# An attention and feed-forward kernel on one core: first loads in halves, tile 0 in halves, V first, hand-chosen PSUM banks and a new work list

## The chip, the core and the metric

The kernel runs on one core of a Trainium2 chip. The metric is the device time of one execution in microseconds, from the start to the end of the program on the chip; lower is better. A core has a matrix engine (TensorE, PE in the profile; PEld is its weight load), VectorE (DVE), ScalarE (ACT), GpSimd (POOL) and SyncE (SP). Each works through a queue of instructions of its own in order, and waits on semaphores for the others. Sixteen DMA engines move data between the main memory and the on-chip memory SBUF; matrix products land in PSUM.

## What is computed

With x of 2048 rows by 512, everything in bf16 at the inputs:

```python
xn = _layernorm(x, axis=-1)
return x + _A_ref(xn, A_wq, A_wk, A_wv, A_wo, A_beta) + _B_ref(xn, B_w1, B_w2)
```

`_B_ref` is a feed-forward block: `silu(xn @ w1) @ w2`, with 1792 inner columns. `_A_ref` is an attention of 32 heads of width 16 over 4 segments of 512 rows, each with a memory of the segments before:

```python
logits = jnp.einsum('bhqd,bhkd->bhqk', qs, ks) * scale + mask
p = _softmax(logits, axis=-1)
a_dot = jnp.einsum('bhqk,bhkd->bhqd', p, vs)
num = jnp.einsum('bhld,bhde->bhle', pq, M)
den = jnp.einsum('bhld,bhd->bhl', pq, z)[..., None] + 1e-06
o = g * (num / den) + (1.0 - g) * a_dot
M = M + jnp.einsum('bhld,bhle->bhde', pk, vs)
z = z + jnp.einsum('bhld->bhd', pk)
```

`pq` and `pk` are `phi(q)` and `phi(k)`, `phi(t) = t + 1` where t is positive, else `exp(t)`; the outputs of the segments go through `wo`.

## The kernel before, in words

**Tiles.** The 2048 rows are 16 tiles of 128, four to a segment. A row tile is loaded, its mean and variance are taken on VectorE (`ln_sums`, line 286, and `ln_var`, line 289), one over the deviation is a square root on ScalarE (line 303) and a reciprocal on VectorE (line 306) for tiles 0 to 3, a power on GpSimd (lines 297 and 300) for four tiles at once later on. `ln_norm` (line 315) writes the normed tile. It is then transposed into `xnT`: tiles 0 to 3 on TensorE against an identity (`turn_mm`, line 845) with a copy out of PSUM (`turn_copy`, line 851), tiles 4 to 15 by a transposing DMA that SyncE issues (`turn_far`, line 857).

**Products.** k, q and h (the inner feed-forward layer) of a segment are made transposed, 128 of their columns by 512 rows: four passes over the inner dimension of 512. `dense` and `dense_mm` make them in pieces, so that the list can put other work between: for segments 0 and 1 a product has 4 pieces, for 2 and 3 it has 2. In segment 0, `dense` cuts each product into two halves of 256 rows (two pieces each), so that the first half needs only tiles 0 and 1. V is made row tile by row tile (`v_mm`). `product` (lines 336 and 338) issues a pass as one matmul of the whole 128 by 128 array, or as four of 128 rows by 32 columns side by side, when its neighbours are of that tiling.

**Attention.** A "score block" S is 8 to 16 matmuls of 16 or 32 rows (line 724) into four PSUM banks `psS`, and one exponential on ScalarE over 128 by 2048 (line 730), then masks on GpSimd (line 744). There are 72, and one buffer `psS`, so the next block's matmuls wait for the exponential of the one before. E and O (`weigh`, line 791) multiply the weights by V. k needs a copy (line 376) and a split into odd and even heads (`k_split` on GpSimd, or `k_fast`, lines 392 and 393, on VectorE and ScalarE) before the first scores, q a copy (line 399). The other four PSUM banks are a pool with four buffers that take turns (`bank`).

**Output.** `out_mm` adds up 18 passes for an output tile (14 of the feed-forward block, 4 of the attention), in wholes, halves (`oc`), quarters (`od`), and for the last tile in column halves (`oh`); `store` (line 621) and `half_store` (line 668) add x and send the result off.

**Order.** All of this is issued from one list of words, `ORDER`, written out by hand, 1349 words: each word is a function and its arguments (`v0.0.2` is segment 0, tile 0, piece 2 of V; `S0` a score block; `Nv1` the norm of tile 1 on VectorE; `X1.1` its transposes; `Xa1.1` and `Xv2.1` copies on ScalarE and VectorE; `xc`, `xd`, `xq`, `xi` the steps of the statistics; `busy44` 44 fillers, matmuls of zeros that have no use in the result; `tb` a first exponential on one column; `ka`, `kv`, `qa`, `qv`, `va`, `vv` copies on ScalarE or VectorE; `xl` loads of x for the output). The words of one engine run on it in the order of the list. The loads ahead of the list are issued by SyncE and ScalarE in the order of the program: SyncE x tiles 0 and 2, wv in two halves, wk, wq, x tiles 4 to 7, w1 in two halves, x tiles 8 to 11, 12 to 15, beta; ScalarE x tiles 1 and 3.

The tiling of a product's neighbours decides its form, by this table in the last loop:

```python
TILED = {"S": "rows", "E": "cols", "O": "cols", "s": "cols", "m": "cols", "X": "whole", "busy": "whole"}
```

Of the kernel before, what the change touches and what calls it, by code (L numbers as in the profile page):

```python
# [22 lines left out]
S7 xs11 xg8.4 v1.2.0 v1.2.1 v1.2.2 v1.2.3 vv1.2 h0.1.2 h0.1.3 ha0.1 E0  # L23
S5 h0.4.0 h0.4.1 hv0.1 Ev0 h0.4.2 h0.4.3 v1.1.0 v1.1.1 fv0.2 v1.1.2 v1.3.0 fp0.3 ha0.4 v1.1.3 vv1.1
S11 hv0.4 q1.2.0 q1.2.1 q1.2.2 v1.3.1 kind fa0.1 q1.2.3 qv1.2 v1.3.2 v1.3.3 vv1.3 Nv8 XD8 O0 lw0 kp0.3 fv0.0 Ov0
S6 fa0.3 k1.2.0 k1.2.1 k1.2.2 h0.5.0 h0.5.1 h0.5.2 q1.1.0 h0.5.3 ha0.5 k1.2.3 kv1.2 q1.1.1 q1.1.2 hv0.5
S8 h0.7.0 q1.1.3 qv1.1 h0.6.0 h0.6.1 h0.6.2 h0.6.3 ha0.6 fv0.3 E1 Ev1 k1.0.0
S9 hv0.6 h0.7.1 h0.7.2 h0.7.3 Om0 ha0.7 k1.0.1 k1.0.2 kp1.2 q1.0.0 q1.0.1 q1.0.2 fp0.1 Nv9 XD9 xs12 k1.0.3 kv1.0 kp1.0
S10 h0.8.0 hv0.7 h0.8.1 h0.8.2 h0.8.3 ha0.8 h0.9.0 h0.9.1 q1.0.3 t0.3 Nv10 XD10 h0.9.2 h0.9.3 qv1.0
S13 hv0.8 O1 Ov1 xs15 v1.0.0 v1.0.1 v1.0.2 ha0.9 v1.0.3 vv1.0 h0.10.0 h0.10.1 bmask  # L30
S12 k1.1.0 k1.1.1 k1.1.2 t0.2 k1.1.3 kv1.1 h0.10.2 h0.10.3 ha0.10 hv0.9 h1.0.0 Om1 h1.0.1 h1.0.2
# [62 lines left out]
def kernel(  # L94
# [13 lines left out]
    nc = tc.nc  # L108
# [211 lines left out]
    def bank(shape, dtype, name):  # L320
        return pp.tile(shape, dtype, name=name, tag="pb")
# [621 lines left out]
```

## Time and profile before

| what | value |
|---|---|
| time, median of three runs | 220.31 us (220.21 to 221.13) |
| span of the profiled execution, first to last instruction | 218.2 us |
| the profiled execution's own time | not given; the median is 2.1 us above its span |
| TensorE busy | 210.9 us, 97% |
| ScalarE busy | 184.1 us, 84% |
| VectorE busy | 181.3 us, 83% |
| GpSimd busy | 127.4 us, 58% |
| first score block (line 724), start | 11.95 us |
| first exponential of scores (line 730), start | 12.40 us |
| exponentials of scores | 72 of 1.878 us |

A row of the profile's timeline gives the start, the duration, the engine, the line of the kernel, the instruction, what it writes and reads, the shape and how many instructions are merged in it; in brackets stands how long the engine was idle before and what ended that. A row of the stretches gives the window, its length, then for each of TensorE, its weight loads, VectorE, ScalarE and GpSimd the busy time and the number of instructions, then the clock granted to TensorE, the share of the DMA engines and the GB/s moved. The ends of matmuls are modelled and overlap, so a busy TensorE is not one at its peak.

### The profile page before, as it was taken

To read this page: it belongs to the slowest core of one execution; us is meant where nothing else is said; L and a number is where in the kernel's file an instruction comes from. 1 tells how busy PE (TensorE), PEld (TensorE's weight loads), DVE (VectorE), ACT (ScalarE), POOL (GpSimd) and SP (SyncE) were. 2 spreads that over 40 slices of the span, in tenths; PEclk is the share of its full clock that TensorE was granted. 3 is DMA by queue.
4 is the path that set the end of the run, shared out by engine and by line. 5 is a ranking of instruction groups with operands and counts; after the bars stand their busy time and mean duration, and the time that the engine had idled before them with its cause. 6 is when DMAs were issued, how large, how long until landed. Compare 5 with 4: busy or idle time off the path is not lost.

```text
span 218.2 us, 9267 instructions
## 1 busy us (share of the span) xinstructions
PE 210.9 (97%) x3982; PEld 116.1 (53%) x4006; DVE 181.3 (83%) x370; ACT 184.1 (84%) x173; POOL 127.4 (58%) x203
## 2 busy tenths in 40 slices
PE   7899999999999999999999999999999999999994
PEld 7666656655544544455444545445464544465653
DVE  6899999999799899667979886887979897858844
ACT  3799999999999999999999999999989998942000
POOL 6067676789568984697766436962787473410000
PEclk9999999999999999999999999999999999999999
DMA  6996249322200430541125131420042120412223
GB/s 183 344 375 160 51 125 243 74 53 53 51 5 17 157 71 10 117 95 40 49 67 83 54 97 28 74 77 6 0 132 73 52 73 13 131 32 79 84 66 98
DMA packets 33273, 19.60 MB, mean 90 GB/s; under 512 B 14672, under 2 KB 33232, under 8 KB 33232
## 3 DMA queue, kind: packets, MB, share of 16 engines
q1 hardware_dynamic: 30608, 16.39, 28.7%
q10 hardware_dynamic: 2624, 2.62, 3.8%
q8 instruction: 31, 0.51, 1.0%
q14 instruction: 10, 0.08, 0.1%
HBM read 9.96 MB, written 2.10 MB: 55 GB/s over the span
## 4 chain that ended last, share of the span: by engine, by line
PE 92%; DMA 3%; ACT 2%; issue 1%; SPq 1%; DVE 0%
PE ps L336 26%; PE psO L338 17%; PE ps L338 16%; PE psS L724 11%; PE psO L336 9%; PE psV L791 8%; PE psS L338 4%; DMA wk_sb<-in_A_wk_dram 3%; ACT Pb L730 2%; PE psM L452 1%; SPq L169 0%; SPq L158 0%; PE ps L509 0%; ACT th L492 0%; DVE o_half L668 0%
## 5 line engine op out<-in xcount | busy, mean ns | idle before, releaser
L730 ACT ACTIVATE Pb<-psS 128x2048 bf16<-128x2048 f32 x72 | 135.2, 1878 | 4.7 <-PE psS L724 2.4
L744 POOL TENSOR_SCALAR_AFFINE_SELECT Pb<-Pb 128x512 bf16<-128x512 bf16 (+2 forms) x88 | 62.3, 718 | 22.4 <-ACT Pb L730 19.6
L497 DVE SCALAR_TENSOR_TENSOR hT<-th,ps 128x512 bf16<-128x512 bf16 x56 | 38.0, 682 | 10.1 <-ACT th L492 9.4
L744 POOL TENSOR_SCALAR_AFFINE_SELECT lows<-Pb 64x512 bf16<-64x512 bf16 (+1 forms) x40 | 24.3, 607 | 32.0 <-ACT Pb L730 24.9
L338 PE MATMUL psO<-w_sb,hT 128*32 128x512 bf16 (+2 forms) x696 | 41.4, 321 | 0.0
L336 PE MATMUL ps<-xnT,w_sb 128*128 128x512 bf16 (+1 forms) x177 | 35.9, 330 | 0.2 <-issue 0.2
L492 ACT ACTIVATE th<-ps 128x512 bf16<-128x512 f32 x56 | 33.0, 594 | 3.5 <-PE ps L338 3.1
L338 PEld LDWEIGHTS <-hT 128*32 128x32 bf16 x864 | 21.5, 96 | 14.6 <-issue 3.1
L338 PE MATMUL ps<-xnT,w_sb 128*32 128x512 bf16 (+1 forms) x408 | 24.8, 349 | 0.0
L724 PE MATMUL psS<-qT,k 32*128 32x64 bf16 (+3 forms) x512 | 23.0, 233 | 0.2
L336 PEld LDWEIGHTS <-w_sb 128*128 128x128 bf16 x178 | 16.4, 98 | 11.9 <-issue 1.2
L336 PE MATMUL psO<-w_sb,hT 128*128 128x512 bf16 (+2 forms) x82 | 20.5, 324 | 0.7 <-issue 0.6
L791 PEld LDWEIGHTS <-Vz 128*32 128x32 bf16 x768 | 16.1, 97 | 9.5 <-issue 0.6
L791 PE MATMUL psV<-Pb,Vz 128*32 128x448 bf16 (+7 forms) x512 | 21.0, 286 | 0.0
L724 PEld LDWEIGHTS <-k 32*128 32x128 bf16 x512 | 9.3, 92 | 21.2 <-issue 20.4
L336 PE MATMUL ps<-xnT,wk_sb 128*128 128x256 bf16 (+1 forms) x63 | 14.4, 326 | 0.4 <-DMA wk_sb<-in_A_wk_dram 0.2
L724 PE MATMUL psS<-qT,kT 16*128 16x448 bf16 (+3 forms) x256 | 14.7, 269 | 0.0
L338 PEld LDWEIGHTS <-w_sb 128*32 128x32 bf16 x408 | 10.3, 96 | 6.7 <-issue 1.7
L621 DVE SCALAR_TENSOR_TENSOR o_out<-psO,x_res 128x512 bf16<-128x512 f32 x14 | 9.4, 679 | 5.0 <-PE psO L338 3.9
L336 PEld LDWEIGHTS <-hT 128*128 128x128 bf16 x92 | 8.5, 98 | 9.6 <-issue 2.1
L828 DVE CAST odd<-psV 128x512 bf16<-128x512 f32 x16 | 11.0, 687 | 2.4 <-PE psV L791 2.4
L338 PE MATMUL psO<-wo_sb,oT 128*32 128x512 bf16 x140 | 12.8, 379 | 0.0
(112 smaller groups left out, 330.0 us busy)
## 6 DMA issues: line engine op xcount, KB each, us to landing
spr<-rz SPq DMA_DIRECT2D x56, 64.0 KB
x_res<-in_A_x_dram SPq DMA_DIRECT2D x16, 128.0 KB
out_dram<-o_out SPq DMA_DIRECT2D x15, 128.0 KB
w_sb<-in_B_w_dram SPq DMA_DIRECT2D x2, 896.0 KB
w_sb<-in_B_w_dram ACTq DMA_DIRECT2D x1, 1792.0 KB
x_hi<-in_A_x_dram SPq DMA_DIRECT2D x2, 512.0 KB
wv_sb<-in_A_wv_dram SPq DMA_DIRECT2D x2, 256.0 KB
wk_sb<-in_A_wk_dram SPq DMA_DIRECT2D x1, 512.0 KB
```

The costliest lines, as they stand in the source:

```text
L336: return [nc.tensor.matmul(out, lhsT=lhsT, rhs=rhs, start=start, stop=stop, skip_group_check=True)]
L338: nc.tensor.matmul(out[c : c + 32], lhsT=lhsT[:, c : c + 32], rhs=rhs, start=start, stop=stop, tile_position=(0, c), skip_group_check=True,)
L452: nc.tensor.matmul(psM[32 * g : 32 * g + 32, i, :].rearrange("p (r d) -> p r d", d=DH), lhsT=st["phiK", dt][:, j, 32 * g : 32 * g + 32], r ...
L492: nc.scalar.activation(out=th[:], in_=sts[s]["h", ft][:, :], func=AF.Tanh, scale=0.5)
L497: nc.vector.scalar_tensor_tensor(out=st["hT"][:, ft, :], in0=st.pop(("th", ft))[:], scalar=1.0, in1=st.pop(("h", ft))[:, :], op0=ALU.add, ...
L621: out = nc.vector.scalar_tensor_tensor(out=o_out[:], in0=st.pop(("psO", j)), scalar=0.5, in1=st["x", j][:], op0=ALU.mult, op1=ALU.add)
L724: nc.tensor.matmul(psS[:, g, c : c + q2 - q1], lhsT=keys[rows], rhs=st["qT"][rows, dt, q1:q2], start=True, stop=True, tile_position=(32 * ...
L730: exp = nc.scalar.activation(out=blocks(Pb, b).rearrange("p y g c -> p g y c"), in_=psS[:, :, :].rearrange("p g (y c) -> p g y c", c=BLOCK ...
L744: over[id(Pb)].append(nc.gpsimd.affine_select(out=out, in_=in_, compare_op=ALU.is_ge, fill=0.0, base=base, pattern=[[0, out.shape[1]], [1, ...
L791: nc.tensor.matmul(psV[32 * g : 32 * g + 32, q0 : q0 + nq].rearrange("p (y c) -> p y c", y=weights.shape[2]), lhsT=Vzs[s % 2][:, kt, 4 * d ...
L828: copy(out=odd[:], in_=sts[s].pop(("psV", 1))[:, :])
```

## The change

The x tile 0 is loaded as two halves of 64 rows, one from SyncE's queue and one from ScalarE's; wv and wk as two halves of the inner dimension, likewise. The first square root on ScalarE (which brings its table in) is issued between ScalarE's x tiles 1 and 3. The zeroing of `lows_all` goes from VectorE to GpSimd, as a word of the list. Tile 0 is normed in two halves of 256 columns (`Nh`), each transposed by two matmuls into a bank of its own (`Y`) and copied on its own (`Ya`). Only k0.0, k0.1 and q0.0 are still cut into halves of rows; the other 19 products of segment 0 go over all 512. The pool of four turning PSUM buffers becomes four fixed banks, and `BANKS` says digit by digit which one the next user gets. The list is new throughout: V of tiles 0 and 1 stands ahead of k, `busy44` and `busy6` become one `busy34`, V of tiles 0 and 1 is copied on ScalarE, the score blocks come in another order (3, 1, 0, 4, 2, 6, 5, 17, ...), and the fillers between them are dealt out anew.

```diff
 ORDER = """
-ones0 ones1 zeros xc0 xd0 xc1 xq0 xi0 Nv0 busy44 xd1 xq1 xc2 busy6 xi1 X0.1 xd2 xq2 Nv1 X1.1 Xa0.1 v0.0.0 v0.0.1 v0.0.2 xs3 xi2 Nv2 xq3 xi3 v0.0.3 X2.1 Xa1.1 k0.1.0 tb Nv3 X3.1 Xv2.1 k0.1.1 Xv3.1 vv0.0 odd omask k0.0.0 k0.0.1 k0.0.2 k0.0.3 ka0.0 fp0.0 q0.0.0 kf0.0 q0.0.1 q0.0.2 q0.0.3 k0.1.2 k0.1.3 q0.2.0 v0.2.0 qa0.0 xs5 ka0.1 kp0.1
-S0 v0.1.0 v0.1.1 xs6 xs7 q0.2.1 v0.2.1 v0.2.2 v0.2.3 vv0.2 fa0.0 k0.2.0 k0.2.1 k0.2.2 xs4 xg4.4
-S2 q0.2.2 q0.2.3 qv0.2 k0.2.3 kv0.2 fp0.2 fa0.2 v0.1.2 v0.1.3 vv0.1 Nv5 Nv6 XD6 q0.1.0 q0.1.1 q0.1.2 q0.1.3 qv0.1
-S1 h0.0.0 h0.0.1 h0.0.2 xs10 h0.0.3 v0.3.0 v0.3.1 v0.3.2 v0.3.3 ha0.0 vv0.3 q0.3.0 kp0.2 hv0.0
-S3 h0.3.0 h0.3.1 q0.3.1 q0.3.2 h0.3.2 tanh XD5 h0.3.3 k0.3.0 Nv7 XD7 q0.3.3 qv0.3 k0.3.1 xs8 ha0.3
-S4 Nv4 h0.1.0 k0.3.2 h0.1.1 hv0.3 XD4 h0.2.0 h0.2.1 h0.2.2 h0.2.3 ha0.2 xs9 k0.3.3 kv0.3 hv0.2
...
+xc0 xd0 xc1 xq0 xi0 xd1 Nh0.0 busy34 Y0.0 xq1 Nh0.1 Y0.1 xc2 ones1 lowz xi1 xd2 Ya0.0 v0.0.0 Ya0.1 v0.0.1 xq2 Nv1 X1.1 v0.0.2 v0.0.3 xi2 Nv2 xc3 X2.1 Xa1.1 v0.1.0 v0.1.1 v0.1.2 v0.1.3 xd3 odd xq3 k0.1.0 Xv2.1 v0.2.0 ones0 va0.0 va0.1 v0.2.1 xi3 Nv3 X3.1 Xv3.1 k0.1.1 k0.0.0 xs7 k0.0.1 tb k0.0.2 k0.0.3 ka0.0 fp0.0 kf0.0 q0.0.0 q0.0.1 q0.0.2 q0.0.3 qa0.0 k0.1.2 k0.1.3 ka0.1 fp0.1 kp0.1 xl1.2 v0.2.2 v0.2.3 xs6
+S3 q0.3.0 q0.3.1 k0.2.0 k0.2.1 k0.2.2 vv0.2 k0.2.3 xs4 kv0.2 xs5 xg4.4 k0.3.0 zeros q0.1.0 fa0.0 fv0.0 fp0.2 k0.3.1
+S1 v0.3.0 k0.3.2 k0.3.3 kv0.3 q0.1.1 v0.3.1 kp0.2 q0.3.2 fa0.3 Nv6 v0.3.2 q0.1.2 q0.1.3 qv0.1 Nv4
+S0 XD6 kp0.3 Nv5 h0.3.0 h0.3.1 v0.3.3 vv0.3 XD5 q0.3.3 qv0.3 h0.0.0 h0.0.1 h0.3.2 h0.3.3 ha0.3 h0.0.2
+S4 q0.2.0 hv0.3 q0.2.1 h0.0.3 ha0.0 xs12 q0.2.2 xl0.0 q0.2.3 h0.2.0 v1.2.0 v1.2.1 h0.2.1
+S2 qv0.2 v1.2.2 Nv7 hv0.0 v1.2.3 h0.1.0 vv1.2 h0.1.1 h0.1.2 h0.1.3 ha0.1 xs10 hv0.1 h0.2.2 h0.2.3 ha0.2 v1.1.0 v1.1.1
+S6 v1.1.2 v1.1.3 fa0.2 XD4 vv1.1 XD7 k1.2.0 lw1 q1.2.0 q1.2.1 q1.2.2 q1.2.3 hv0.2 xs9 qv1.2 E0
...
 """
+
+BANKS = "01230130212123023021320320120210213203212302102301003120310130120120331313113121330303033030031302122303103130301301011001010130120100100131021032102022020220223311310331010002"
@@
-    pp = ctx.enter_context(tc.tile_pool(name="pp", bufs=4, space=bass.MemoryType.PSUM))
+    pp = ctx.enter_context(tc.tile_pool(name="pp", bufs=1, space=bass.MemoryType.PSUM))
@@
-    load_x(nc.sync, 0, 1)
+    zraw = cpool.tile([P, L // 2], BF16, name="zraw")
+    nc.vector.memset(zraw[:], 0.0)
...
+    for eng, r0 in ((nc.sync, 0), (nc.scalar, P // 2)):
+        rows = slice(r0, r0 + P // 2)
+        eng.dma_start(out=x_lo[rows, 0, :], in_=x_flat[rows, :])
     load_x(nc.scalar, 1, 1)
     load_x(nc.sync, 2, 1)
+    nc.scalar.activation(out=spare[:], in_=zraw[:, 0:1], func=AF.Sqrt)
     load_x(nc.scalar, 3, 1)
...
-    load_w(nc.sync, wv_sb, A_wv, 0, 2)
-    load_w(nc.sync, wv_sb, A_wv, 2, 4)
-    load_w(nc.sync, wk_sb, A_wk, 0, 4)
+    for w_sb, W in ((wv_sb, A_wv), (wk_sb, A_wk)):
+        load_w(nc.sync, w_sb, W, 0, 2)
+        load_w(nc.scalar, w_sb, W, 2, 4)
     load_w(nc.sync, wq_sb, A_wq, 0, 4)
@@
-    nc.vector.memset(lows_all[HP:P], 0.0)
+    def make_lows():
+        nc.gpsimd.memset(lows_all[HP:P], 0.0)
@@
-    def bank(shape, dtype, name):
-        return pp.tile(shape, dtype, name=name, tag="pb")
+    pool = [pp.tile([P, L], F32, name=f"pb{i}") for i in range(4)]
+    turns = iter(BANKS)
+    def bank():
+        return pool[int(next(turns))][:, :]
@@
+    HALVED = {('k', 0), ('k', 1), ('q', 0)}
     def dense(s, name, w_sb, i, part):
-        if s == 0:
+        if s == 0 and (name, i) in HALVED:
@@
+    def norm_half(t, h):
+        cols = slice(h * D // 2, (h + 1) * D // 2)
+        xn[t, h] = work.tile([P, D], BF16, name="xn_t", tag="x_res", bufs=4)[:, 0 : D // 2]
+        nc.vector.tensor_scalar(
+            out=xn[t, h], in0=xs(t, t + 1)[:, 0, cols], scalar1=mv_all[:, t, 0:1], scalar2=rstd_all[:, t, 0:1],
+            op0=ALU.subtract, op1=ALU.mult,
+        )
+    def turn_half(t, h):
+        ptr = xn["ptr", t, h] = bank()[:, 0:P].bitcast(BF16).rearrange("p (d c) -> p d c", d=2)
+        xn_t = xn.pop((t, h))
+        for d in range(2):
+            nc.tensor.transpose(ptr[:, d, :], xn_t[:, d * P : (d + 1) * P], ident[:])
+    def half_copy(t, h, copy):
+        copy(out=xnT[:, 2 * h : 2 * h + 2, t * P : (t + 1) * P], in_=xn.pop(("ptr", t, h)))
```

More of the change, by code (lines that the diff above doesn't have):

```diff
@@ L26 @@
[L26 to L31, printed above, removed]
@@ new lines @@
+S13 hv0.9 fv0.3 Nv9 v1.0.0 v1.0.1 v1.0.2 t0.3 h0.10.3 v1.0.3 vv1.0 h1.0.0 h1.0.1 h1.0.2 q1.3.0 ha0.10 q1.3.1
+S12 hv0.10 Nv11 XD11 q1.3.2 q1.3.3 k1.1.0 k1.1.1 k1.1.2 h1.10.0 qv1.3 h1.0.3 ha1.0 h1.10.1 k1.1.3 kp1.2 kv1.1 kp1.1
+S11 XD9 tanh E2 h1.10.2 h1.10.3 hv1.0 ha1.10 h1.3.0 h1.3.1 h1.3.2 h1.3.3 Ev2
+S15 h0.12.0 h0.12.1 h0.12.2 lw0 kind m0.2 h0.12.3 hv1.10 mv0.2 k1.3.0 O2 Om1 ha0.12
+S16 Ov2 hv0.12 ha1.3 k1.3.1 k1.3.2 k1.3.3 q2.1.0 k2.2.0 k2.2.1 kv1.3
+S14 hv1.3 q2.1.1 qv2.1 q2.3.0 q2.3.1 kv2.2 qv2.3 h0.13.0 h0.13.1 h0.13.2 ga1.1
@@ L185 @@
     )
-    zraw = cpool.tile([P, L // 2], BF16, name="zraw")
-    nc.vector.memset(zraw[:], 0.0)
-    spare = cpool.tile([P, 1], F32, name="spare")
-    nc.scalar.activation(out=spare[:], in_=zraw[:, 0:1], func=AF.Sqrt)
     ident = cpool.tile([P, P], BF16, name="ident")
@@ L896 @@
     pieces = [word.rstrip("0123456789.") for word in words]
-    TILED = {"S": "rows", "E": "cols", "O": "cols", "s": "cols", "m": "cols", "X": "whole", "busy": "whole"}
+    TILED = {"S": "rows", "E": "cols", "O": "cols", "s": "cols", "m": "cols", "X": "whole", "Y": "whole", "busy": "whole"}
     ahead = ["rows"] * (len(words) + 1)
```

147 lines of the change are left out of this document (75 added, 72 removed).

## The prediction

> **What bounds the kernel now.** First the busy shares and the chain that ended last, from the page; then the busy time in four stretches.
>
> ```profile
> span 218.2 us, 9267 instructions
> ...
> PE 210.9 (97%) x3982; PEld 116.1 (53%) x4006; DVE 181.3 (83%) x370; ACT 184.1 (84%) x173; POOL 127.4 (58%) x203
> ...
> PE 92%; DMA 3%; ACT 2%; issue 1%; SPq 1%; DVE 0%
> ```
> ```profile
> 0.00:12.00 12.00, 10.09 (x102) 8.37 (x105) 8.75 (x26) 6.87 (x16) 4.24 (x16) 1.00 0.84 274
> 12.00:192.00 180.00, 177.54 (x3299) 93.28 (x3325) 155.61 (x312) 174.62 (x154) 122.39 (x185) 1.00 0.32 80
> 192.00:215.20 23.20, 23.20 (x595) 14.48 (x584) 16.54 (x32) 2.65 (x5) 0.78 (x2) 1.00 0.24 71
> 215.20:218.20 3.00, 0.06 (x4) 0.00 (x0) 0.42 (x1) 0.00 (x0) 0.00 (x0) 1.00 0.29 91
> ```
>
> The first busy column is TensorE. From 12 us to 215.2 it has work in hand nearly always (177.54 of 180.00, then 23.20 of 23.20); after 215.2 comes a last vector step and a store. ScalarE is as full (174.62) until 192, but then TensorE alone runs on for 23 us, so ScalarE may be some tenths late at no cost. The end is therefore: the time of the first score block, plus the products that are still to do then, plus TensorE's waits, plus a tail of 3.0 us. The change touches mainly the first two. So I read the start line by line (start, duration, engine, what waited).
>
> ```profile
> 3.35 0.69 DVE L286 BATCH_NORM_STATS2 stats<-x_lo 128x6 f32<-128x512 bf16 x1 [0.72 <-DMA x_lo<-in_A_x_dram]
> ...
> 4.36 0.29 ACT L303 ACTIVATE rstd_all<-mv_all,eps 128x1 f32<-128x1 f32 x1 [1.14 <-POOL Zw L272]
> 4.76 0.14 DVE L306 RECIPROCAL rstd_all<-rstd_all 128x1 f32<-128x1 f32 x1
> 4.94 0.41 DVE L315 TENSOR_SCALAR xn_t<-x_lo,mv_all,rstd_all 128x512 bf16<-128x512 bf16 x1
> ...
> 5.36 0.66 DVE L286 BATCH_NORM_STATS2 stats<-x_lo 128x6 f32<-128x512 bf16 x1
> ...
> 5.69 0.39 PE L845 MATMUL ptr<-ident,xn_t 128*128 128x128 bf16 x4
> ...
> 6.47 0.63 ACT L851 COPY xnT<-ptr 128x256 bf16<-128x256 bf16 x2
> ...
> 6.59 0.40 PE L845 MATMUL ptr<-ident,xn_t 128*128 128x128 bf16 x4 [0.52 <-DVE xn_t L315]
> ...
> 6.88 1.04 PE L336 MATMUL ps<-wv_sb,xnT 128*128 128x512 bf16 x3
> ...
> 8.23 1.28 ACT L309 ACT_TABLE_LOAD   x1
> 8.34 0.42 DVE L851 COPY xnT<-ptr 128x512 bf16<-128x512 bf16 x1
> ...
> 8.54 0.39 PE L336 MATMUL ps<-xnT,wk_sb 128*128 128x256 bf16 x2 [0.24 <-DMA wk_sb<-in_A_wk_dram]
> ...
> 10.11 1.04 PE L336 MATMUL ps<-xnT,wq_sb 128*128 128x256 bf16 x8
> ...
> 10.30 0.58 ACT L376 CAST kT<-ps 128x512 bf16<-128x512 f32 x1 [0.58 <-PE ps L336]
> 10.92 0.51 ACT L393 ACTIVATE k<-kT,pm_even 128x256 bf16<-128x256 bf16 x1
> ...
> 11.34 0.56 ACT L399 CAST qT<-ps 128x512 bf16<-128x512 f32 x1
> ...
> 11.51 0.69 DVE L286 BATCH_NORM_STATS2 stats<-x_hi 128x6 f32<-128x512 bf16 x1 [0.23 <-DMA x_hi<-in_A_x_dram]
> ...
> 11.95 0.21 PE L724 MATMUL psS<-qT,k 32*128 32x64 bf16 x4
> ...
> 12.29 0.60 PE L336 MATMUL ps<-wv_sb,xnT 128*128 128x512 bf16 x2
> ...
> 12.40 1.88 ACT L730 ACTIVATE Pb<-psS 128x2048 bf16<-128x2048 f32 x1
> ...
> 14.79 1.88 ACT L730 ACTIVATE Pb<-psS 128x2048 bf16<-128x2048 f32 x1
> ```
>
> The first score block starts at 11.95 and lasts 0.34. Before it TensorE has holes: it waits for normed tiles (6.59), for copies of transposes (6.88) and for wk (8.54).
>
> **The change part by part.** *Loads.* The rows show what two queues do here: with both at work (2.5 to 3.5) 371 GB/s move, with SyncE's alone (4 to 6) 250, later 371 again with larger transfers.
>
> ```profile
> 2.50:3.50 1.00, 1.00 (x12) 1.00 (x11) 0.28 (x2) 0.71 (x2) 1.00 (x2) 1.00 1.12 371
> 4.00:6.00 2.00, 2.00 (x29) 1.90 (x27) 1.93 (x8) 0.59 (x2) 0.28 (x2) 1.00 0.81 250
> 7.00:9.00 2.00, 1.71 (x14) 0.86 (x14) 1.66 (x7) 1.69 (x5) 0.00 (x0) 1.00 1.07 371
> ```
> ```profile
> 29.15 1.88 ACT L730 ACTIVATE Pb<-psS 128x2048 bf16<-128x2048 f32 x1
> 29.16 0.39 ACTq L169 DMA_DIRECT2D w_sb<-in_B_w_dram  x1
> ```
>
> Tile 0 stands ahead of everything in both queues now, instead of sharing the engines with all of tile 1: at 371 GB/s half of a 128 KB tile less is 0.17 us. Between no gain and 0.35 (a whole tile) I take 0.15: statistics at 3.20. ScalarE's queue gets one more transfer ahead of tile 1 (tile 1's statistics come 0.83 after tile 0's, which covers it), and tile 3, half of wv and half of wk behind the first activation; the second pair of rows shows such an issue going out while an activation of 1.88 runs, so it isn't held. SyncE's queue loses half of wv and of wk (0.5 MB) ahead of wq. wk thus lands about 1 us earlier ((371 - 250) GB/s for 2 us is 0.24 MB, or 0.65 us, and the halves run together), but the new list needs it only at about 8.3, so nothing hangs on it. The Trainium skill speaks against this part: "DMA: Bandwidth & Descriptors", section "Rules for kernel authors", says that two transfers to disjoint halves of the partitions serialize on the same engines and that spreading them over queues brings no bandwidth. The 250 against 371 disagrees here; by the rule the 0.15 falls away and the sum is 219.5.
>
> *Tile 0 in halves, new order of the start.* From 3.20, with the distances of the rows above: sqrt 4.21, reciprocal 4.61, first half normed at 4.85 (0.28, between a 0.14 step and the 0.41 of a whole tile), transposed at 5.2 (now no filler stands ahead, since 34 at 0.107 end at 4.75), copied 5.5 to 5.85, V of tile 0 from 5.9 instead of 6.88. Tile 1: statistics of tile 2 stand ahead of its norm as before, so its transposes come at 6.55, as before (6.59). Then V0's second half to 7.2, tile 2's transposes, V1 from 7.4 to 8.3, k0.1 first part, tile 2's copy on VectorE 8.1 to 8.5, V2's first half to 9.0, tile 3 transposed at 9.1, copied to 9.95, k0.1.1, k0.0 to 10.45 and drained at 10.6. ScalarE's queue has sqrt of tile 3 (8.0), two V copies (0.6 each, moved here from VectorE; they keep ScalarE to 9.3), the table load and its 0.2 (to 10.75), then the k copy: 10.75 instead of 10.30, though the product is done at 10.6. From that copy to the first score block it is 11.95 - 10.30 = 1.65, as before, for the same copies in the same order: **first score block at 12.40**, 0.45 later; its exponential follows at 12.9, behind one more k copy of 0.5 to 0.6. VectorE's share of the k split waits behind tile 7's statistics (x_hi landed at 11.5 before); 1 us earlier by the faster loads it costs nothing, without that up to 0.3.
>
> The zero memset of 1.2 us moves to GpSimd, idle until 10.98; beside its memsets the norms may stretch, as these rows show for tiles normed beside GpSimd work (524 against 405): 0 to 0.1 each, two on the path; taken as 0, left to the range.
>
> ```profile
> L315 DVE TENSOR_SCALAR xn_t<-x_hi,mv_all,rstd_all 128x512 bf16<-128x512 bf16 x8 | 4.1, 524 | 0.0
> ...
> L315 DVE TENSOR_SCALAR xn_t<-x_lo,mv_all,rstd_all 128x512 bf16<-128x512 bf16 x4 | 1.6, 405 | 0.1
> ```
>
> *What is done by then.* Ahead of the first score block stand 18 pieces of 512 columns in the old list (v0.0, k0.1, k0.0, q0.0, q0.2.0, v0.2.0) and 24 in the new (V of tiles 0, 1, 2, k0.1, k0.0, q0.0). A piece of this kind costs
>
> ```profile
> 186.35 1.03 PE L336 MATMUL ps<-xnT,w_sb 128*128 128x512 bf16 x4
> ```
>
> (1.03 - 0.38)/3 = 0.217 us, so 6 more are **-1.30**.
>
> *Whole columns.* Of 22 dense blocks of segment 0, 19 are no longer cut in two: 4 passes at 0.217 are 0.867 instead of 8 at (1.04 - 0.273)/7 = 0.110, 0.877: 19 x 0.01 = **-0.2** (bounds 0 and -0.4).
>
> *New list and banks behind it.* Both lists hold the same products, 72 score blocks, and by the pieces' rule the same 144 switches between TensorE's tilings, with as many halves and quarters of output products. So the products that remain are equal but for the above. What can differ is waiting. ScalarE's pace at the start is 2.4 us a score block (14.79 - 12.40, an exponential and a shorter step); the new list puts 9, 9, 9, 9 and 10 pieces (1.95 to 2.17) between the first six, with 0.34 for the block and 0.1 on entry: no wait of TensorE, as before. The new place to look at is k1.2.0, the first to need all of tiles 4 to 7: five blocks and 48 pieces behind the first block, at 12.40 + 48 x 0.217 + 6 x 0.44 = 25.4; the old list had its first such use eight blocks on.
>
> ```profile
> 18.33 6.26 SPq L857 DMA_TRANSPOSE xnT<-xn_t  x4
> ```
> ```profile
> 19.50:20.50 1.00, 1.00 (x14) 0.90 (x11) 0.96 (x3) 0.98 (x2) 0.93 (x2) 1.00 0.67 131
> ```
>
> The four far transposes were issued until 24.6, 12.65 behind the first score block; the first, issued at 18.33, moved its bytes mostly between 19.5 and 20.5, so the last landed at about 25.9. With the same distance it would land at 26.35 and cost 0.95. But VectorE has less ahead of the last norm now: from the first score block on three statistics, nine copies and four norms instead of five, eight and four: two statistics less (0.69 and a small step of some 0.15 each) and one copy more, at most as dear as a statistic, about 1.0 us less. So 25.35; I take **+0.1** (0 to 0.95). The four banks chosen by hand only change which release a product waits for; with 177.54 of 180.00 busy there is at most 2.5 us to gain or, for all that the rows show, to lose; I take 0.
>
> Sum: 0.45 - 1.30 - 0.2 + 0.1 = -0.95. On the span, 218.2 to 217.2. The profiled execution's own time isn't given; with the median, 2.1 us lie around its span (220.31 - 218.2), so **219.3 us**.
>
> **The rivals.** (1) *TensorE's clock rises later.* The fillers show it:
>
> ```profile
> 1.10:4.85 3.75, 3.74 (x36) 3.75 (x37) 1.00 0.80 230
> 4.90:5.65 0.75, 0.75 (x17) 0.75 (x14) 1.00 0.67 219
> ```
>
> 36 fillers in 3.75 us, then about 14 in 0.75: half clock until 4.87, though the clock column says 1.00. The new list has 34 fillers, ending at 4.75, then a hole. If the rise is missed until about 8.3, V0, V1 and twelve transposes (2.4 us at full clock, 3.1 available) run at half: 0.85 late behind them, 0.55 to 0.9 at the first score block: 219.9 to 220.2. The Trainium skill, "TensorE: Matmul & The Clock Gate", Part 1, gives a free-running window of some 3.4 us that must be busy; 3.65 us of fillers hold one only if it lies well. Against: before, the clock rose 3.77 after the first filler, 0.1 behind where the new fillers end.
>
> (2) *Slower: the far transposes late.* If VectorE falls behind (it was busy 155.61 of 180) every microsecond that the last of them lands behind 25.4 is one of TensorE. At 26.35 the gain is gone (220.2); from 26.5 the change loses; at 28.5, three norms and copies' worth of queue later, 222.4. For: VectorE's queue is in order and serves them behind copies that wait for products. Against: the sum above.
>
> (3) *The loads don't come earlier.* Statistics at 3.35, x_hi at 11.5: +0.15 and +0.3: 219.75.
>
> (4) *The new list waits less in the stream.* Of the 2.46 us without TensorE work between 12 and 192, a third to a half (0.8 to 1.2) goes: 218.3.
>
> **How the numbers follow.** Forecast 0.48 (218.8 to 219.8), (1) 0.11, (2) 0.16, of which 0.10 beyond 221.4, (3) 0.12, (4) 0.13. The range leaves out the far half of (4) and most of (2): 218.4 to 220.9. A half per cent, 1.1 us, is about what a measurement can tell from none: faster (below 219.2) takes (4) and somewhat over half of the forecast, 0.40; slower (above 221.4) 0.12; within, 0.48.
>
> **What would show it.** First statistics at about 3.2; V of tile 0 at 5.9; TensorE without a hole over 0.4 from 6.5 to 12.4; the first score block at 12.4 with 24 pieces behind it; the first exponential at 12.9; no wait at k1.2.0 near 25.4; the tail 3.0. A first score block behind 12.9, a filler pitch that leaves transposes at half clock, or holes of TensorE between 20 and 30 make it wrong.

## The result, and the profile after

The kernel after took 235.14 us (median of 6, 233.40 to 235.46), the kernel before 220.44 beside it (220.21 to 221.13): a ratio of 1.064, 95% interval 1.061 to 1.068. It is 6.4% slower; the prediction was 219.3. The profiled execution took 235.0. All medians below are of fast executions (new_start leaves out its one slow execution, 225.23 us, which is the one that was profiled). First the busy shares and the chain from the page after:

```profile
span 233.3 us, 9024 instructions
...
PE 217.3 (93%) x3869; PEld 108.8 (47%) x3869; DVE 183.5 (79%) x368; ACT 186.3 (80%) x175; POOL 133.4 (57%) x204
...
PE 14%; DVE 9%; DMA 5%; issue 2%; SPq 2%; ACT 1%; DVEq 0%
```

The work is nearly the same: no engine is busy more than 6.4 us longer, in 15.1 us more. The chain that ended last can be followed back only to 155.47 us here, so its shares add up to 33%; of these TensorE has 14, VectorE 9 and transfers 5, where before TensorE has 92 of 99. So in the last third TensorE waits, mostly for VectorE and for transfers. The busy time by stage shows where time goes in the whole span (first busy column TensorE, "PEclk" the granted clock):

```profile
0.00:12.00 12.00, 8.70 (x64) 6.27 (x65) 5.80 (x21) 5.18 (x13) 5.58 (x14) 0.86 0.84 268
12.00:208.60 196.60, 187.86 (x3288) 89.39 (x3289) 162.51 (x318) 178.87 (x160) 127.18 (x189) 1.00 0.28 75
208.60:230.00 21.40, 20.72 (x524) 13.18 (x516) 14.81 (x30) 2.20 (x5) 0.69 (x1) 1.00 0.20 59
230.00:233.30 3.30, 0.00 (x0) 0.00 (x0) 0.37 (x2) 0.00 (x0) 0.00 (x0) 0.91 0.38 119
```

Two losses: the start is slow and at a lower clock, and the middle has 8.7 us without TensorE, where before had 2.5 in 180. Whom TensorE waited for, the longest totals first (us in total, times, longest), after and then before:

```profile
PE pb L348 <- DVE hT L509: 1.5, 2, 1.2
PE pb L346 <- DMA wv_sb<-in_A_wv_dram: 1.2, 1, 1.2
...
PE pb L346 <- DVE Vz L418: 1.1, 2, 0.9
...
PE pb L803 <- POOL Pb L756: 0.5, 1, 0.5
```
```profile
PE psO L336 <- issue: 1.0, 6, 0.2
```

Behind the first score block every entry of after's list but the 0.5 for GpSimd is a wait for VectorE, some 8.4 us in all. Before has no gap over 0.16 us in its stream, and nearly all of these end at "issue", where the trace shows no cause. (Its trace also has 24 matmuls fewer than weight loads, 3982 against 4006, so some of these gaps may be missing records.)

The last column of the first row of the stages (268 GB/s) is no better than before's 274. The start after, line by line (start, duration, engine, what waited):

```profile
2.30 0.42 SPq L170 DMA_DIRECT2D wv_sb<-in_A_wv_dram  x1
...
2.97 0.39 ACTq L170 DMA_DIRECT2D wv_sb<-in_A_wv_dram  x1
...
3.41 0.69 DVE L293 BATCH_NORM_STATS2 stats<-x_lo 128x6 f32<-128x512 bf16 x1 [2.37 <-DMA x_lo<-in_A_x_dram]
...
7.16 0.80 PE L346 MATMUL pb<-wv_sb,xnT 128*128 128x512 bf16 x2 [1.21 <-DMA wv_sb<-in_A_wv_dram]
7.75 0.63 PE L876 MATMUL pb<-ident,xn_t 128*128 128x128 bf16 x4
...
9.45 1.71 PE L346 MATMUL pb<-wv_sb,xnT 128*128 128x512 bf16 x4
...
11.80 1.28 ACT L316 ACT_TABLE_LOAD   x1
...
14.90 0.40 PE L736 MATMUL psS<-qT,k 32*128 32x192 bf16 x8
...
15.35 1.88 ACT L742 ACTIVATE Pb<-psS 128x2048 bf16<-128x2048 f32 x1
...
206.73 1.88 ACT L742 ACTIVATE Pb<-psS 128x2048 bf16<-128x2048 f32 x1 [0.40 <-PE psS L736]
```

TensorE is done with tile 0's transposes at 5.95, and V of tile 0 ends a hole of 1.21 us, held up by wv. Its first two pieces need the half of wv in SyncE's queue, issued at 2.30 where before issues it at 1.70; the half in ScalarE's queue is needed by the next two. Soon after, the clock is down, as the granted clock by the microsecond (column before the last two) says:

```profile
6.00:7.00 1.00, 0.00 (x0) 0.10 (x1) 0.90 (x6) 0.75 (x3) 0.49 (x1) 1.00 0.96 312
7.00:8.00 1.00, 0.84 (x5) 0.45 (x5) 1.00 (x2) 0.00 (x0) 0.00 (x0) 0.71 1.06 329
8.00:9.00 1.00, 1.00 (x6) 0.48 (x5) 0.29 (x3) 0.58 (x3) 0.00 (x0) 0.50 1.05 358
9.00:10.00 1.00, 1.00 (x7) 0.70 (x6) 0.30 (x1) 0.84 (x3) 0.00 (x0) 0.50 1.10 387
10.00:11.00 1.00, 1.00 (x5) 0.33 (x4) 0.60 (x3) 0.00 (x0) 0.00 (x0) 0.59 1.08 382
```

0.58 + 1 + 1 + 0.82 = 3.4 us at half speed: four V pieces take 1.71 instead of 1.03. The Trainium skill, "TensorE: Matmul & The Clock Gate", Part 1, says that half clock follows an idle window of some 3.4 us and full clock comes back only after a busy window of as much. The trace agrees with the second, with 3.4 us at half speed; the holes ahead of it are only 1.0 and 1.2 us.

Three numbers sort every run below: the start of the first exponential, the time from it to the start of the last, and the rest to the end of the span.

| profile | first | to the last | rest | span |
|---|---|---|---|---|
| before | 12.40 | 178.04 | 27.76 | 218.2 |
| after | 15.35 | 191.38 | 26.57 | 233.3 |
| difference | +2.95 | +13.34 | -1.19 | +15.1 |

The visible holes (8.7 us, against 2.5) are less than the 13.34: a matmul of 512 columns counts as 0.38 busy, though four in a row take 1.03, so the first 0.16 of a wait behind one counts as work. The rest of the difference is not taken apart here.

So three questions: what delays the first exponential, what stretches the stream by 13, and why the work done early saves only 1.2 at the end.

### The profile page after: what moved, and what is told of

Same layout as the page of the kernel before. It is cut to its first block, busy times and chain, and to the rows that moved or that the text cites. A ratio compares the mean times of both kernels' runs of the same rounds, so it can differ in the third digit from the quotient of the medians.

```text
span 233.3 us, 9024 instructions
## 1 busy us (share of the span) xinstructions
PE 217.3 (93%) x3869; PEld 108.8 (47%) x3869; DVE 183.5 (79%) x368; ACT 186.3 (80%) x175; POOL 133.4 (57%) x204
## 5 line engine op out<-in xcount | busy, mean ns | idle before, releaser
L742 ACT ACTIVATE Pb<-psS 128x2048 bf16<-128x2048 f32 x72 | 135.1, 1877 | 11.7 <-PE psS L736 10.8
L756 POOL TENSOR_SCALAR_AFFINE_SELECT Pb<-Pb 128x256 bf16<-128x256 bf16 (+2 forms) x88 | 64.7, 745 | 27.8 <-ACT Pb L742 25.0
L509 DVE SCALAR_TENSOR_TENSOR hT<-th,pb 128x512 bf16<-128x512 bf16 x56 | 37.6, 677 | 7.8 <-ACT th L504 7.5
L504 ACT ACTIVATE th<-pb 128x512 bf16<-128x512 f32 x56 | 32.8, 595 | 7.4 <-PE pb L348 5.0
L348 PE MATMUL pb<-w_sb,hT 128*32 128x512 bf16 (+2 forms) x652 | 38.7, 317 | 0.0
L346 PE MATMUL pb<-xnT,w_sb 128*128 128x512 bf16 x124 | 34.1, 379 | 2.6 <-DVE qT L411 0.9
L348 PE MATMUL pb<-xnT,w_sb 128*32 128x512 bf16 x400 | 27.2, 380 | 0.8 <-DVE M L479 0.4
L346 PE MATMUL pb<-w_sb,hT 128*128 128x512 bf16 (+2 forms) x103 | 25.6, 335 | 0.0
L803 PE MATMUL pb<-Pb,Vz 128*32 128x448 bf16 (+7 forms) x512 | 21.4, 287 | 0.9 <-POOL Pb L756 0.5
L346 PE MATMUL pb<-xnT,wq_sb 128*128 128x512 bf16 (+1 forms) x50 | 13.1, 363 | 0.9 <-DVE Vz L418 0.9
L346 PE MATMUL pb<-xnT,wk_sb 128*128 128x512 bf16 (+1 forms) x54 | 13.0, 347 | 0.0
```

The costliest lines, as they stand in the source:

```text
L346: return [nc.tensor.matmul(out, lhsT=lhsT, rhs=rhs, start=start, stop=stop, skip_group_check=True)]
L348: nc.tensor.matmul(out[c : c + 32], lhsT=lhsT[:, c : c + 32], rhs=rhs, start=start, stop=stop, tile_position=(0, c), skip_group_check=True,)
L504: nc.scalar.activation(out=th[:], in_=sts[s]["h", ft][:, :], func=AF.Tanh, scale=0.5)
L509: nc.vector.scalar_tensor_tensor(out=st["hT"][:, ft, :], in0=st.pop(("th", ft))[:], scalar=1.0, in1=st.pop(("h", ft))[:, :], op0=ALU.add, ...
L742: exp = nc.scalar.activation(out=blocks(Pb, b).rearrange("p y g c -> p g y c"), in_=psS[:, :, :].rearrange("p g (y c) -> p g y c", c=BLOCK ...
L756: over[id(Pb)].append(nc.gpsimd.affine_select(out=out, in_=in_, compare_op=ALU.is_ge, fill=0.0, base=base, pattern=[[0, out.shape[1]], [1, ...
```

## The experiments

All ran beside the kernel before. Median and ratio with its interval come first; "first", "to the last" and "rest" are those of the table.

### Start and list apart

*new_start*: the new start, then before's order.

```
- ORDER: new start, new list
+ ORDER: new start, then before's words that are left, in before's order; banks as they come free
```

> The kernel after up to the first score block (its loads, its halves of tile 0, its V first), and behind it the remaining words in the order of the kernel before, with banks given in the order in which they come free. Theory 1 (the order behind the first score block is what costs some 13.5 us, the start costs its own 2.95 less the 1.3 + 0.2 of work done earlier): 221.5 to 222.5, TensorE waits over 0.15 us in the stream of about 1 us in all. Rival A (the late start knocks the stream out of step, so any stream behind it waits): 230 or more, with waits of 5 us or more. Rival B (no room: a mix of both): between.

222.22, 1.011 (1.007 to 1.016). First 17.73, to the last 177.81, rest 27.96. Theory 1 holds, rival A falls: though the profiled execution starts its exponentials 2.38 later than after's, the stream behind them is as short as before's.

*old_start*: before's start, then the new list, before's rotating banks.

```
- ORDER: old start, old list
+ ORDER: old start without q0.2.0, then the new list's words that are left
```

> The kernel before up to the first score block, without its q0.2.0 and with the words of the new list's start that are still to do ahead of the new list's next block; behind it the new list as it stands; the banks by rotation as in the kernel before. Theory 1 (the new list behind the start costs about 13.5 us by itself): 232 to 235, with the waits of TensorE behind VectorE's copies near the same words (phiQT, hT, oT behind the spreads). Rival A (the list only suffers from the start): 220 to 223.

231.09, 1.051 (1.048 to 1.053). First 14.64, to the last 188.85, rest 26.01. The list alone costs 10.8 us between the exponentials, with the old loads, the old start and banks in rotation: neither the start nor the hand-chosen banks are needed for it.

### The loads and the clock

*old_loads*: after with x's tiles 0 to 3, wv and wk loaded as before.

```
- x tile 0, wv, wk in halves on SyncE and ScalarE; table load ahead of tile 3's issue
+ x tiles 0, 2, wv, wk on SyncE; x tiles 1, 3 on ScalarE; then the table load
```

> The kernel after with the loads of x's tiles 0 to 3, wv and wk as before (tile 0 whole on SyncE's queue, wv in two transfers and wk in one on SyncE's). Theory 2 (V0 waits 1.21 us because half of wv stands behind three tiles and a table load's issue in ScalarE's queue): V0 at about 6.0 to 6.3, first score block at 13.9 or earlier, 234.0. Rival C (two queues bring no bandwidth and wv lands at the same time either way): V0 at 7.0 to 7.2 and 235.1. Rival D (wk is late instead, 8.5 before): first score block 14.9 or later.

231.17, 1.051 (1.047 to 1.054): better than after by 4.0 us in the medians, 3.0 by the ratios, more than expected. First 13.09, to the last 189.94, rest 25.97; V0 starts at 6.29, as theory 2 has it. The reason that theory 2 gives is not the right one, though: what V0 waited for in after was the half in SyncE's queue.

*more_fillers*: after with both holes of TensorE filled.

```
- busy34 Y0.0 xq1 Nh0.1 Y0.1 xc2
+ busy46 Y0.0 xq1 Nh0.1 Y0.1 busy20 xc2
```

> The kernel after with 46 instead of 34 fillers ahead of tile 0's transposes and 20 more between them and V of tile 0, into the two holes of TensorE (4.53 to 5.53 and 5.95 to 7.16). Theory 3 (the clock falls back at 7.41 because TensorE stood still for 2.2 of the 3.4 us before): full clock from 4.0 on, transposes of tile 1 in 0.3 to 0.4 instead of 0.63, first score block at 13.1 to 13.6 instead of 14.9, 233.5. Rival E (the work behind 7.4 is bound by loads, norms and copies, not by the clock): clock kept, first score block at 14.6 or later, 235.

233.22, 1.060 (1.057 to 1.063), 1.9 below after in the medians, 1.0 by the ratios. The granted clock stays at 1.00, tile 1's transposes take 0.39, first is 14.11: between these two executions the clock is worth 1.24 us at the first exponential. The first score block starts at 13.66, just behind the 13.6 expected, because V0 still waits for the second half of wv (0.54 us, at 8.24).

*before_new_loads*: before with the new loads alone.

> The kernel before with only the loads of x's tile 0, wv and wk changed as in the change (halves on two queues, the table load ahead of tile 3's issue). Theory 2 (the second half of wv stands in ScalarE's queue and shares the engines with wk, wq and x's later tiles on SyncE's): V of tile 0 waits until 7.2 or later instead of 6.88, and the first score block comes 0.3 to 1.5 later: 220.5 to 221.9. Rival C (the loads gain as predicted, only the new list needs wv too early): 219.9 to 220.3 or faster.

222.22, 1.012 (1.007 to 1.016). First 14.35, to the last 177.95: 1.95 lost ahead of the first exponential, more than theory 2 expected, and nothing behind it. The waits of this kernel, in order of time:

```profile
7.57 0.59 PE L338 MATMUL ps<-wv_sb,xnT 128*128 128x512 bf16 x2 [0.47 <-DMA wv_sb<-in_A_wv_dram]
8.67 0.59 PE L338 MATMUL ps<-wv_sb,xnT 128*128 128x512 bf16 x2 [0.51 <-DMA wv_sb<-in_A_wv_dram]
...
10.95 1.27 PE L338 MATMUL ps<-xnT,wk_sb 128*128 128x256 bf16 x10 [1.02 <-DMA wk_sb<-in_A_wk_dram]
```

The second pair of V0's pieces, which needs the half in ScalarE's queue, waits once more, and wk, which was to come 1 us earlier, is late by another 1.02.

*w_halves_only* (after, wv and wk in halves, x whole) and *x_halves_only* (after, tile 0 in halves, wv and wk as before):

> The kernel after with x's tiles 0 to 3 loaded whole as before, and only wv and wk in halves on two queues (ScalarE's behind the table load). Theory 2 (the split of wv is what delays V0 and drops the clock): V0 at 7 or later, first score block at 14 or later, 234 to 235. Rival F (the split of tile 0 is to blame): as old_loads, V0 at 6.3, 231.

> The kernel after with only tile 0 of x in halves on two queues; wv, wk and the place of the table load as before. Theory 2b (halves of tile 0 alone already cost something, since all later transfers are issued 0.6 later in both queues): V0 at 6.5 to 7, 232 to 233.5. Rival (only the split of wv and wk costs): as old_loads, 230.5 to 232.

233.10, 1.058 (1.054 to 1.062), and 232.53, 1.056 (1.053 to 1.058), where old_loads has 1.051 and after 1.064. Each half of the edit seems to cost something, though both intervals overlap a little with that of old_loads (1.047 to 1.054). First w_halves_only, then x_halves_only:

```profile
7.98 1.01 PE L344 MATMUL pb<-wv_sb,xnT 128*128 128x512 bf16 x2 [1.15 <-DMA wv_sb<-in_A_wv_dram]
```
```profile
5.53 0.61 PE L864 MATMUL pb<-ident,xn_t 128*128 128x128 bf16 x4 [0.62 <-DVE xn_t L855]
7.06 1.01 PE L346 MATMUL pb<-wv_sb,xnT 128*128 128x512 bf16 x2 [0.92 <-DMA wv_sb<-in_A_wv_dram]
```

With wv and wk in halves alone, SyncE issues the first half of wv at 1.70, as before, and V0 still waits for it until 7.98 instead of 6.29: the other half, issued by ScalarE at 1.78, and wk are now on their way beside it. With tile 0 in halves alone, wv is on SyncE's queue again, but some 0.6 us later (2.29), behind one more issue, and V0 waits until 7.06.

The first exponential of that execution is 2.15 later than in old_loads (15.24 against 13.09). This is not the price of the delay alone: tile 0's transposes, which come ahead of V0, already take 0.61 (0.42 in after and old_loads), so the matmuls had never reached full speed. The profiles of no_side_dma and neither below show the same with the loads of old_loads (transposes 0.61, first 14.95, in the first; half speed until past 10 us, first 15.08, in the second; their fillers multiply ones instead of zeros). So when full speed comes differs from execution to execution, and how much of the 1.4 us between the medians is the delay and how much the clock is not shown.

### Why the new list waits

One place of the kernel after in full: VectorE from 20 us, then GpSimd, then TensorE.

```profile
20.59 0.67 DVE L411 CAST qT<-pb 128x512 bf16<-128x512 f32 x1
21.18 1.99 DVE L322 TENSOR_SCALAR xn_t<-x_hi,mv_all,rstd_all 128x512 bf16<-128x512 bf16 x2
23.10 0.68 DVE L418 CAST Vz<-pb 128x512 bf16<-128x512 f32 x1
```
```profile
21.20 0.66 POOL L756 TENSOR_SCALAR_AFFINE_SELECT lows<-Pb 64x512 bf16<-64x512 bf16 x1
21.93 1.10 POOL L756 TENSOR_SCALAR_AFFINE_SELECT Pb<-Pb 128x1024 bf16<-128x1024 bf16 x1
```
```profile
22.64 0.25 PE L736 MATMUL psS<-qT,kT 16*128 16x192 bf16 x4
23.83 0.38 PE L346 MATMUL pb<-xnT,wq_sb 128*128 128x512 bf16 x1 [0.93 <-DVE Vz L418]
```

The words are `Nv4 ... Nv5 ... v0.3.3 vv0.3 ... q0.2.0`. Two norms that take 0.4 each when alone take 1.99 and end at 23.17, just behind the second mask (23.03). Behind them stands the copy `vv0.3`, and q0.2.0 takes the bank which that copy frees. TensorE stands still for 0.93 though nothing in its own list is amiss. The other kind of place, VectorE and then TensorE at 124:

```profile
124.61 0.60 DVE L601 TENSOR_TENSOR oT<-spr,oraw 128x512 bf16<-128x512 bf16 x1 [2.24 <-DMA spr<-rz]
125.13 0.67 DVE L509 SCALAR_TENSOR_TENSOR hT<-th,pb 128x512 bf16<-128x512 bf16 x1
```
```profile
125.86 0.62 PE L348 MATMUL pb<-wv_sb,xnT 128*32 128x512 bf16 x8 [1.19 <-DVE hT L509]
```

Here VectorE stands 2.24 us for a spread of weights, with a bank-freeing step queued behind it. Two runs, both made from old_loads, take one cause away each, a third both, and a control does so in before. All leave out work, as their expectations say.

```
  no_select:    - select(firsts[:, :, 0:P], ...)      + select(firsts[:, 0:1, 0:P], ...)
  no_side_dma:  - the transfers of move_sums, spread  + return; return xnT[:, dt, 0:L]
```

> The kernel old_loads with GpSimd's masks of the weights cut to one block or one head's rows each (the 88 selections of Pb, 64.7 us of GpSimd's 133; the causal mask is thus not complete); all else as it was. Theory 1b (norms, sums and products of VectorE that stretch from 0.5 - 0.7 to 1.0 - 1.6 us beside GpSimd's work push the copies behind them): 4 to 5 us of the waits go, 226 to 227.5, and the mean of those operations falls. Theory 1a: 230 to 232. Rival G (waits come from the order of TensorE's own work and the banks): 230 to 232 here and in no_side_dma.

> The kernel old_loads without the transfers of sums and weights: the moves of row sums into zraw and the 56 spreads are left out, and the multiplications that read a spread read the transposed x instead (zraw starts at 1 so that all reciprocals stay finite), so part of the memory term is not computed; every instruction of VectorE stays. Theory 1a (VectorE stands for these transfers, 4.4 + 2.3 us for spreads and 2.2 + 1.7 for sums in the profile after, and TensorE behind it): 3 to 4 us of the waits go, 227 to 228. Theory 1b (VectorE is late because its operations are stretched beside GpSimd's): within 1 us of old_loads, 230 to 232.

> Both of these left out of old_loads at once. Theory 1 in either form: most waits go, 222 to 224.5. Rival G: 229 or more.

> Both left out of the kernel before, as a control of what the missing work is worth by itself. All theories: TensorE hardly waits there, so 219 to 220.5; if it falls further, what neither gains has to be read against that.

| run | median | ratio (95%) | to the last |
|---|---|---|---|
| old_loads | 231.17 | 1.051 (1.047-1.054) | 189.94 |
| no_side_dma | 229.32 | 1.041 (1.038-1.045) | 187.36 |
| no_select | 225.47 | 1.025 (1.023-1.027) | 183.45 |
| neither | 222.22 | 1.011 (1.009-1.013) | 181.60 |
| before_neither | 219.82 | 0.998 (0.997-1.000) | 177.90 |

Without the masks 6.5 us of the stretched 11.9 go, without the side transfers 2.6, without both 8.3; the same work left out of before is worth 0.1. Theory 1b carries most of it and more than expected, 1a less; rival G falls. GpSimd's masks held TensorE directly for only 0.5 us in old_loads, so most of the 6.5 came by way of VectorE. The 3.6 that stay without both are not explained. What shrank, by groups (busy, mean ns of one), first in old_loads, then in no_select:

```profile
L443 DVE SCALAR_TENSOR_TENSOR pk<-ex,pos 128x512 bf16<-128x512 bf16 x12 | 11.6, 966 | 0.0
...
L320 DVE TENSOR_SCALAR xn_t<-x_hi,mv_all,rstd_all 128x512 bf16<-128x512 bf16 x8 | 5.7, 722 | 0.9 <-POOL rstd_all L305 0.9
```
```profile
L443 DVE SCALAR_TENSOR_TENSOR pk<-ex,pos 128x512 bf16<-128x512 bf16 x12 | 8.7, 721 | 0.0
...
L320 DVE TENSOR_SCALAR xn_t<-x_hi,mv_all,rstd_all 128x512 bf16<-128x512 bf16 x8 | 4.4, 565 | 0.8 <-POOL rstd_all L305 0.6 <-DMA xnT<-xn_t 0.2
```

The Trainium skill, "SBUF — State Buffer", section "SBUF: two separate sides", says that VectorE (with two SBUF inputs, or in a fast mode) and GpSimd take turns at a shared pair of ports, and that the later one waits for the whole instruction. The trace agrees: the second norm ends 0.14 behind the second mask.

Yet before pays for it too, though less in these two groups (its `pk` takes 699 on average, its norms 524): without masks and transfers VectorE's busy time falls from 181.3 to 174.7 there, from 183.6 to 174.7 in old_loads, and before gains 0.2 us by it. The difference is, as I read the lists, what stands behind it. If each product gets the bank that came free first, 6 of before's some 170 products follow the copy that frees their bank within one piece of TensorE's work; in the new list 22 do. And one `zv` (`zv3.0`) stands right behind its `z` there. No run changes these distances alone.

*copies_first*: could VectorE's order alone mend it? In old_loads, 30 norms, statistics, sums and merges went behind the next one or two bank-freeing copies.

```
- qv0.1 Nv4  S0  XD6 kp0.3 Nv5 h0.3.0 h0.3.1 v0.3.3 vv0.3 XD5 q0.3.3 qv0.3
+ qv0.1      S0  XD6 kp0.3     h0.3.0 h0.3.1 v0.3.3 vv0.3 Nv5 XD5 q0.3.3 qv0.3 Nv4      (and so on)
```

> The kernel old_loads with VectorE's queue rearranged in the stream and nothing else: some 30 norms, statistics, sums, merges and multiplications (Nv, xs, fv, gv, Om, zv, dv, mw, r) put behind the one or two next copies that free a bank, wherever that copy's product was done before; TensorE's order unchanged, banks given as they come free. Theory 1 (TensorE stands because the copy that frees its next bank is queued behind VectorE work that is stretched beside GpSimd or waits for a DMA): a third to two thirds of the some 11 us of waits go: 224 to 228. Rival G (the waits come from the number of banks or from ScalarE, not from VectorE's order): 230 to 232.

233.52, 1.060 (1.057 to 1.063), to the last 190.42: a miss. The waits at the copies grew less, and others came where the deferred work was itself awaited (1.14 us for a far transpose at 28, 1.32 for a `phiQT` at 136). So this remedy fails, and the run does not confirm the cause; that rests on the waits for VectorE and on no_select and no_side_dma.

### Where the early work goes

*new_start_old_loads*: new_start with the old loads.

> The start of the kernel after (tile 0 normed and transposed in halves, V of tiles 0, 1 and 2 first, whole columns), but with the loads of the kernel before, and behind the first score block the remaining words in the order of the kernel before. Theory 1 with theory 2 (loads and stream order are the two costs; the rest of the start is worth about what the prediction gave it): first score block at 12.6 to 12.9, 218.7 to 219.9 where the kernel before has 219.87 to 220.44. Rival A (more work early only meets ScalarE, which sets the pace of the first score blocks: the run of new_start had waits of TensorE for ScalarE's exponential of 1.18, 0.52 and 0.31): 220 to 221, no gain.

222.04, 1.007 (1.005 to 1.010): theory 1's forecast was too low, rival A fits. First 13.32, to the last 177.95, rest 27.83: all +0.92 of the first exponential stays in the span (219.1), and the 1.5 us of work done early or dropped is not seen. TensorE's line shows where it went:

```profile
15.25 0.40 PE L734 MATMUL psS<-qT,k 32*128 32x64 bf16 x8 [1.01 <-ACT Pb L740]
17.63 0.21 PE L734 MATMUL psS<-qT,k 32*128 32x64 bf16 x4 [0.36 <-ACT Pb L740]
```

The pieces done early had stood between the first score blocks; without them TensorE reaches the second block before the first exponential has freed `psS`. Before has no such wait.

*act_late*: before with six `tb` words ahead of S0, a delay of ScalarE alone.

> The kernel before with six more one-column exponentials on ScalarE ahead of the first score block's exponential (some 0.8 to 1.2 us of ScalarE, nothing on any other engine). Theory S (ScalarE's chain from the first exponential to the last sets the pace, TensorE fills in): the first and the last exponential come 0.8 to 1.2 later and so does the end, 221.0 to 221.7. Rival T (TensorE's work sets the end, as the prediction had it; ScalarE has a few tenths to spare and catches up in 180 us): within 0.4 of the kernel before.

221.13, 1.005 (1.003 to 1.006). First 13.47 (+1.07), last 191.47 (+1.03), span +1.1: as theory S says.

*few_exps_before*, *few_exps_new*: 24 exponentials fewer on ScalarE, in before and in new_start_old_loads.

> The same left out of the kernel before, as control. Theory S with TensorE close behind ScalarE: 218.5 to 220. Rival T: 219.8 to 220.5, no change.

> The kernel new_start_old_loads without the 24 exponentials of the feature map (VectorE takes k and q themselves in their place, so the memory term's features are not computed): some 15 us less on ScalarE, nothing less elsewhere. Theory S: with ScalarE relieved the early work of TensorE shows: 0.7 to 1.5 below few_exps_before. Rival T: it stays 0.9 to 1.6 above few_exps_before, as new_start_old_loads stood above the kernel before.

220.95, 1.002 (1.000 to 1.004), and 222.04, 1.008 (1.005 to 1.011). With 11 us of ScalarE's work gone (184 to 173 busy in before) neither gets faster, and the pair stays 1.1 apart. So it is not the amount of ScalarE's work that sets the pace, though act_late fitted theory S. What fits all four, without a run that tests it alone: TensorE sets the pace of the stream, but each piece keeps its place behind a score block, and the second block cannot start before the first exponential ends. In these runs a delay there was not made up.

*shifted*, *shifted_before*: every score block from the second on put behind 1.5 us more of pieces, so that the gaps are filled again.

```
- S0 v0.1.0 ... xg4.4  S2 q0.2.2 ...
+ S0 v0.1.0 ... xg4.4  q0.2.2 q0.2.3 ... q0.1.1  S2 ...      (so for all 71)
```

> The kernel new_start_old_loads with every score block from the second on moved behind 1.5 us more of TensorE's pieces in the list (the pieces done early had stood between the first blocks), nothing else. Theory T2 (TensorE's work sets the end; the early work was lost in waits for the first exponentials, since each later piece kept its place behind a score block): the waits of 1.18, 0.52 and 0.31 go, 1.2 to 1.8 below new_start_old_loads (222.04): 220.2 to 220.9, level with the kernel before or a little below. Theory S (ScalarE's chain): no gain or up to 1.5 slower, 222 to 223.5.

> The kernel before with the same move of its score blocks, as control: every exponential from the second on comes 1.5 us later against TensorE's work. Theory T2: within 0.5 of the kernel before (the first gap gets longer, no work is added). Theory S: 1 to 1.5 slower.

273.20, 1.240 (1.236 to 1.244), and 273.01, 1.240 (1.236 to 1.244): both expectations missed by 50 us, and the question isn't answered by it. In the control TensorE's products with the weights wait 17.4 us, and ScalarE waits 52.4 for score blocks:

```profile
L730 ACT ACTIVATE Pb<-psS 128x2048 bf16<-128x2048 f32 x72 | 135.1, 1876 | 53.0 <-PE psS L724 52.4
...
L791 PE MATMUL psV<-Pb,Vz 128*32 128x448 bf16 (+7 forms) x512 | 23.2, 292 | 17.4 <-POOL Pb L744 13.4 <-DVE hT L497 4.1
```

E and O now stood right behind the block whose exponential and mask they read. That refilled gaps would return the 1.5 us is therefore argued, not shown. No version that beats both kernels came out of these runs.

## Why the prediction was wrong

- **Loads.** "I take 0.15: statistics at 3.20" failed: 3.41, no gain; rival (3) was right in kind. The larger miss was that the step followed wk only. The first half of wv was issued 0.6 us later than before (2.30), behind the extra half of tile 0, and other transfers ran beside it; V0, forecast at 5.9, waited until 7.16. The rule on queues which the prediction set aside because of 250 against 371 GB/s held: with the new loads the first 12 us move 268 GB/s against 274.
- **Clock.** Rival (1) had the mechanism at 0.11 and put the damage at 0.55 to 0.9 by a late rise. In the profiled execution the rise came in time; the hole behind it took the clock away again, for 3.4 us, 1.24 at the first exponential. In x_halves_only, no_side_dma and neither the same 34 fillers did miss it, as rival (1) says, and the first exponential came 1.9 to 2.2 behind that of old_loads. The argument against this rival rested on one execution: before's 50 fillers take 4.74 us there, and 4.54 to 5.51 in the seven profiles of that start.
- **First score block** "at 12.40": 14.90. Between two executions, old loads mend 2.26 of the first exponential's 2.95; that the remaining 0.69 lies near the 0.5 forecast says little when the start alone varies by more.
- **Work done by then**, "-1.30": wrong as a saving. With the old order it turns into waits for the first exponentials (1.01 and 0.36). In the new list the rest behind the last exponential is 1.19 shorter; that this comes from the early work is not shown.
- **Whole columns**, "-0.2": no run isolates it.
- **New list and banks** is the step that failed: "with 177.54 of 180.00 busy there is at most 2.5 us to gain or, for all that the rows show, to lose; I take 0". A busy share bounds what a new order can gain. It says nothing of what it can lose: the stream from the first exponential to the last got 13.34 us longer, 7.9 of it as visible waits of TensorE for VectorE. Rival (2) named VectorE's in-order queue but priced it at the far transposes alone, which came in time; the price is paid at copies that free a bank, all along the list. Rival (4) fell; the 2.46 us of which it wanted a part are gaps of 0.16 at most.

## What to carry to other kernels

A stream that is 98% busy with in-order queues is held together by distances, so a new order has to be priced place by place: for each product, which copy frees its bank, what stands ahead of that copy in its engine's queue, and how long that takes beside GpSimd or behind a transfer. Work done early pays only if something later can move into the gap it leaves. Before splitting a load over queues, ask what else then runs beside the half that is needed first.

## What the runs showed of the hardware

- The granted clock is not the whole story. In x_halves_only it reads 1.00 from 3 to 12 us, while products run at half speed (2 V pieces in 1.06 instead of 0.59, four transposes in 0.63 instead of 0.39):

```profile
8.29 1.06 PE L346 MATMUL pb<-wv_sb,xnT 128*128 128x512 bf16 x2
9.14 0.63 PE L876 MATMUL pb<-ident,xn_t 128*128 128x128 bf16 x4
```
```profile
8.00:9.00 1.00, 1.00 (x7) 0.60 (x6) 0.34 (x4) 0.46 (x2) 0.00 (x0) 1.00 1.01 337
```

- Full speed does not come at a fixed time: the same 34 fillers take 3.43 us in one profile (after) and 3.81 in another (x_halves_only), where matmuls stay at half speed until past 10 us.
- A transfer that shares the engines lands later: the first half of wv, issued at 1.70 or 1.71, is there for V0 at 6.29 in old_loads and at 7.98 in w_halves_only, where the other half goes out beside it instead of behind it.
- 1.5 us of displacement of the score blocks in a list of some 1300 words cost 53 us.
